# Attention probabilities by values in float32 with two heads in column halves, and one pool of four PSUM banks

## The chip, the cores and the metric

The kernel runs on one core of a Trainium2 chip. A core has five engines that run side by side, each with its own queue taken in order: TensorE (PE in the profile, its weight loads PEld), VectorE (DVE), ScalarE (ACT), GpSimd (POOL) and SyncE (SP), which here only issues transfers. Matmul results land in PSUM, eight banks of 512 float32 a partition; everything else lives in SBUF, 128 partitions. The metric is device time of one execution, in microseconds (us).

## What is computed

Threshold attention over 8 batches, 8 heads, 576 positions of 64 channels, and behind it a feed-forward part on the 512 channels of a position. Cut to what matters:

```python
scores = scale * q @ k.T                       # per head, 576 x 576
thresh = max(scores, axis=-1) - tau
p = where(scores >= thresh, exp(scores - max), 0)
attn = p / (sum(p) + 1e-9)
x = attn @ v                                   # heads side by side: 8 x 576 x 512
xk = mu_k * x + (1 - mu_k) * x_prev            # x_prev: the position before
xr = mu_r * x + (1 - mu_r) * x_prev
k = maximum(xk @ w_k, 0)                       # 512 -> 1024
out = sigmoid(xr @ w_r) * ((k * k) @ w_v)
```

The weights arrive as float64 words and are converted on the chip.

## The kernel before

**Number formats.** Outside batch 0 a float32 operand is split into a rounded part (`hi`, float32r) and the rest (`lo`), and a product is taken as hi x hi + hi x lo + lo x hi in the faster float32r form. The first eight jobs are `plain`: float32 throughout.

**Attention.** A job is a pair of heads of one batch (`hp`); batch 0 is cut into two rounds of four half jobs. `operands` (L397) loads q and k, scales q, splits (ScalarE L433, GpSimd L439) and stacks them by transfers into `st1`, `st2`; the values are loaded as `vraw` and split into `vs` (ScalarE L481, GpSimd L489). A unit is two query tiles of 128 rows of one head (kind P), or the last 64 rows of both heads (kind T, with the block-diagonal operand `bd`, GpSimd L528). `softmax` (L576) takes each query tile (128 x 576 scores, two banks of the tag `s`) through maximum (DVE L599), threshold (ACT L607), exponent (ACT L615), mask with row sum (DVE L623), inverse (DVE L633, L634) and scaling (POOL L648) into `p`. `turn_pair` (L693) and `turn_last` (L756) transpose `p` on TensorE (L670, banks of the tag `pt`) and evict each bank twice: `upper` rounds on ScalarE (L681) into `phi`, `lower` subtracts on VectorE (L687) into `plo`. `attend` (L809) multiplies by `vs` for one head: 9 matmuls with 128 output columns of the array (L860), where one half of the output holds the product with the rounded values and the other the product with their rest. ScalarE copies one half (L872) and VectorE adds the halves into `xT` (L880), or `xE` for the last 64 rows (L894). Plain jobs multiply in float32 (L823).

**Feed-forward.** `ffn_chunk` (L916) takes 256 positions at a time, 18 chunks. It mixes (difference POOL L958, scale ACT L966, sum POOL L975, rounding ACT L981, rest POOL L989), multiplies by `w_k` (L1011), takes relu, square, rounding and rest into `k2` (L1019 to L1034, through the tile `r`), multiplies by `w_r` (L1053), takes the sigmoid (L1061), multiplies by `w_v` (L1075), gates (DVE L1081) and stores. Its products and the output of `attend` use banks of the tag `w`.

**Weights.** `weight` (L317) converts each of 20 pieces: absolute value (ACT L340), clip (POOL L348), three bit operations (DVE L362, L369, L379), rounding (ACT L386) and rest (POOL L390), with `xT[1]` as scratch.

**Order.** Every step is recorded with an engine, an estimated duration, what it reads and writes, and a key. `Plan.order` (L108) simulates the engines: at each step it takes the ready step that can start first, ties by the smaller key, and writes out the order in which all are issued. Attention's TensorE steps have keys 1000 lower, so the feed-forward part fills what attention leaves. A tile of a tag takes that tag's buffers in turn: the n-th waits for the release of the one `bufs` before it. PSUM's eight banks: `s` two tiles of two banks, `pt` two, `w` two.

## Time and profile before

| | us |
|---|---|
| median of 3 runs (lowest, highest) | 1181.38 (1179.02, 1182.25) |
| the profiled execution | 1178.11 |
| its span, first to last instruction | 1176.3 |

| engine | busy us | share of the span |
|---|---|---|
| PE | 1084.4 | 92% |
| PEld | 932.4 | 79% |
| ACT | 906.4 | 77% |
| DVE | 860.7 | 73% |
| POOL | 748.7 | 64% |

The mean granted clock of TensorE is 0.978 of full speed. A line of the profile's groups reads: line of the kernel, engine, operation, tile written <- tiles read, shapes, count | busy us, mean ns of one | idle time of that engine just before them and what ended it. Matmuls are pipelined, and the records' ends are modelled, so the rate of a stream of matmuls is read from start to start, not from the duration of a record.

### The profile page before, as it was taken

Reading aid. Unit: us, or ns where it says so; the run is one execution under the profiler, and the core shown is the slowest. Engines: PE = TensorE matmul, PEld = TensorE weight load, DVE = VectorE, ACT = ScalarE, POOL = GpSimd, SP = SyncE. Lnnn points to the kernel's source line nnn. Section 1 sums busy time; section 2 is a strip of 40 time slices with the busy share of each in tenths; the row PEclk is TensorE's granted clock in tenths of the full one; section 3 lists DMA queues with packets and bytes.
Section 4 is the critical chain, followed back from the end, with each engine's and each line's share of the span. In section 5 each row is a group of like instructions: output and inputs, shape, how many; then the busy total and the mean of one; then the engine's idle time right before and its main releaser. Section 6 shows DMA issues by size and latency. Waiting matters only on the chain.

```text
span 1176.3 us, 20089 instructions
## 1 busy us (share of the span) xinstructions
PE 1084.4 (92%) x6728; PEld 932.4 (79%) x6728; DVE 860.7 (73%) x2013; ACT 906.4 (77%) x1918; POOL 748.7 (64%) x854
## 2 busy tenths in 40 slices
PE   6788899997999889997999999999999999998998
PEld 4455678886988778986988888979788888887897
DVE  4678767889778877888878797878787787887100
ACT  4678678887779788887888887878788888875643
POOL 1889865656766476646675766656667676653661
PEclk9789899999999999999999999999999999998999
DMA  6552203434443324244343342434434334220000
GB/s 240 165 206 82 42 22 89 100 105 104 97 113 93 96 57 113 73 94 114 86 114 96 102 108 47 108 82 97 104 96 108 84 82 114 69 56 19 9 28 18
DMA packets 36806, 106.82 MB, mean 91 GB/s; under 512 B 5984, under 2 KB 5984, under 8 KB 36704
## 3 DMA queue, kind: packets, MB, share of 16 engines
q1 hardware_dynamic: 36704, 105.54, 34.5%
q8 instruction: 54, 0.88, 0.3%
q14 instruction: 48, 0.39, 0.1%
HBM read 44.70 MB, written 9.44 MB: 46 GB/s over the span
## 4 chain that ended last, share of the span: by engine, by line
PE 50%; ACT 16%; DVE 16%; POOL 11%; issue 5%; DMA 2%; SPq 0%; POOLq 0%; DVEq 0%; ACTq 0%
PE w L1011 11%; PE s L566 8%; PE pt L670 8%; PE w L1075 7%; PE w L1053 6%; PE w L860 6%; DVE p L623 5%; POOL p L648 4%; ACT p L615 3%; ACT phi L681 3%; DVE plo L687 3%; DVE sm L599 3%; PE w L823 2%; PE s L544 2%; DVE phi L687 2%
## 5 line engine op out<-in xcount | busy, mean ns | idle before, releaser
L648 POOL TENSOR_SCALAR p<-p,sm 128x576 f32<-128x576 f32 x288 | 216.8, 761 | 222.0 <-DVE sm L634 202.7
L681 ACT ACTIVATE phi<-pt 128x512 fp32r<-128x512 f32 (+6 forms) x528 | 227.4, 458 | 65.2 <-PE pt L670 60.8
L623 DVE SCALAR_TENSOR_TENSOR p<-s,sm,p 128x576 f32<-128x576 f32 x288 | 232.8, 815 | 59.1 <-ACT p L615 53.5
L1011 PE MATMUL w<-xk,wk 128*128 128x256 f32 x1728 | 252.3, 291 | 2.3 <-POOL xk L989 1.1
L670 PE MATMUL pt<-ident,p 128*128 128x128 f32 x1312 | 216.7, 281 | 39.0 <-POOL p L648 28.5
L599 DVE TENSOR_REDUCE sm<-s 128x1 f32<-128x576 f32 x288 | 211.7, 751 | 49.9 <-PE s L544 28.9
L1011 PEld LDWEIGHTS w<-xk,wk 128*128 128x128 f32 x1728 | 226.8, 194 | 5.9 <-issue 1.9
L670 PEld LDWEIGHTS pt<-ident,p 128*128 128x128 f32 x1312 | 155.6, 142 | 85.3 <-POOL p L648 52.5
L1075 PE MATMUL w<-wv,k 128*128 128x512 f32 x864 | 221.2, 398 | 0.2 <-ACT sg L1057 0.2
L615 ACT ACTIVATE p<-s,sm 128x576 f32<-128x576 f32 x288 | 211.9, 736 | 1.1
L687 DVE TENSOR_TENSOR plo<-pt,phi 128x512 fp32r<-128x512 f32 x280 | 172.4, 632 | 54.7 <-ACT phi L681 52.4
L1075 PEld LDWEIGHTS w<-wv,k 128*128 128x128 f32 x864 | 155.3, 189 | 28.6 <-ACT sg L1057 0.4
L860 PE MATMUL w<-phi,vs 128*128 128x320 f32 (+1 forms) x560 | 157.0, 303 | 2.0 <-ACT r L1019 1.4
L607 ACT ACTIVATE sm<-sm,small 128x1 f32<-128x1 f32 x288 | 83.9, 291 | 60.9 <-DVE sm L599 59.2
L860 PE MATMUL w<-plo,vs 128*128 128x320 f32 (+1 forms) x448 | 124.7, 300 | 2.9 <-DVE plo L687 2.6
L566 PE MATMUL s<-st 128*128 128x288 f32 x448 | 106.1, 318 | 13.3 <-DVE p L623 12.0
L1034 POOL TENSOR_TENSOR k<-r,k 128x512 fp32r<-128x512 f32 x72 | 92.9, 1290 | 38.3 <-ACT k L1024 38.3
L1053 PE MATMUL w<-wr,xk 128*128 128x512 f32 x432 | 115.3, 401 | 0.0
L860 PEld LDWEIGHTS w<-phi,vs 128*128 128x128 f32 x560 | 105.6, 189 | 5.4 <-ACT r L1019 2.0
L566 PE MATMUL s<-st,st 128*128 128x288 f32 x448 | 97.7, 299 | 0.0
L566 PEld LDWEIGHTS s<-st 128*128 128x128 f32 x448 | 71.3, 190 | 32.2 <-DVE p L623 23.3
L439 POOL TENSOR_TENSOR lo<-raw,hi 128x576 fp32r<-128x576 f32 (+1 forms) x56 | 83.6, 1498 | 18.8 <-ACT hi L433 17.3
(78 smaller groups left out, 1636.7 us busy)
## 6 DMA issues: line engine op xcount, KB each, us to landing
raw<-in_qk SPq DMA_DIRECT2D x28, 608.0 KB, 5.0
st<-hi SPq DMA_DIRECT2D x56, 304.0 KB, 3.3
st<-lo SPq DMA_DIRECT2D x56, 304.0 KB, 4.3
vraw<-in_v SPq DMA_DIRECT2D x28, 320.0 KB, 3.1
out<-sg SPq DMA_DIRECT2D x32, 256.0 KB, 2.0
st<-hi SPq DMA_DIRECT2D x56, 144.0 KB, 3.7
st<-lo SPq DMA_DIRECT2D x56, 144.0 KB, 4.1
st<-in_qk SPq DMA_DIRECT2D x8, 608.0 KB, 5.0
```

What stands on the lines that cost most here:

```text
L566: PE.matmul(s.get()[:, z, 0:HS], lt, r.get()[:, k0 + z * HS : k0 + (z + 1) * HS], start=(j == 0), stop=(j == len(prods) - 1),)
L599: lambda sv=sv, col=col: V.tensor_reduce(col(0), sv(), axis=AX.XY, op=ALU.max, negate=True),
L615: lambda sv=sv, pv=pv, col=col: A.activation(pv(), sv(), AF.Exp, bias=col(0)),
L623: lambda sv=sv, pv=pv, col=col: V.scalar_tensor_tensor(pv(), sv(), col(1), pv(), op0=ALU.is_ge, op1=ALU.mult, accum_out=col(2)),
L648: lambda y=y: G.tensor_scalar(p.get()[:, y], p.get()[:, y], sm.get()[:, 3, y : y + 1], 0.0, op0=ALU.mult, op1=ALU.add),
L670: lambda c=c, o=o: PE.transpose(pt.get()[:, c, :], p.get().rearrange("p y s -> p (y s)")[:, o : o + P], ident.get()),
L681: add("ACT", occ, lambda: A.activation(out_(), in_(), AF.Copy), reads=[pt], writes=w, key=key)
L687: lambda: V.tensor_tensor(out_(), in_(), hi_().bitcast(F32), op=ALU.subtract),
L860: lambda j=j, c=c, m=m: PE.matmul(o.get()[:, 0:n], vs.get()[:, c], m.get()[:, c, 0:n], start=(j == 0), stop=(j == len(prods) - 1)),
L1011: PE.matmul(h.get()[:, f], l, r, start=(ct == 0 and i == 0), stop=(ct == NCT - 1 and i == 2))
L1053: PE.matmul(z.get(), l, r, start=(ct == 0 and i == 0), stop=(ct == NCT - 1 and i == 2))
L1075: PE.matmul(vps.get(), l, r, start=(ft == 0 and i == 0), stop=(ft == NFT - 1 and i == 2))
```

## The change

- The split of probabilities and values goes: `phi`, `plo`, `vs`, `upper`, `lower` are replaced by `pm`, `pl` and `v` in float32 for all jobs. `attend` runs once for both heads of a query half: head 0 writes output rows 0 to 63 of one bank (array columns 0 to 63) and head 1 rows 64 to 127, with float32 matmuls that alternate between the heads.
- A P unit is one query tile of both heads. A plain unit's scores are issued for both heads as one step, heads alternating; they write both `s` tiles.
- A transposed bank is evicted once: the first on ScalarE, the second on VectorE (on ScalarE too up to key 40). One eviction on VectorE takes the product to `xT`, one more to `xE`.
- `bd` is filled on ScalarE, the weights' clip is on VectorE, and in the mixing two operations (scale, sum) become one VectorE operation.
- The tags `pt` and `w` become one of four banks. A tile takes any free buffer of its tag, the one free longest, in place of the next in turn. `r` has one buffer in place of two, `raw` two in place of one.
- Some TensorE steps now record a write to the SBUF tile that their result will be evicted to (`pm`, `pl`, `xT`, `k2`, `sg`), so that they wait for its release themselves.
- A job's order is T, 0, 1, 2, 3 (before: P, T, P, P, P).

```diff
-                h = held[b.tag]
-                if len(h) >= b.bufs:
-                    o = h[-b.bufs]
-                    if left[id(o)]:
-                        return None
-                    t = max(t, freed[id(o)] + self.HOP)
+                h = sorted(freed[id(o)] if o else -1.0 for o in held[b.tag] if not (o and left[id(o)]))
+                if len(h) <= m:
+                    return None
+                t = max(t, h[m] + self.HOP)
...
+    EV = ("ACT", 0.49), ("DVE", 0.6)
...
-            "POOL",
-            0.7,
-            lambda: G.tensor_scalar(t(), t(), W_MIN, W_MAX, op0=ALU.max, op1=ALU.min),
+            "DVE",
+            0.46,
+            lambda: V.tensor_scalar(t(), t(), W_MIN, W_MAX, op0=ALU.max, op1=ALU.min),
...
+        raw = job["raw"] = sbuf("raw", [P, W], F32, 2)
...
+        vt = job["v"] = sbuf("v", [P, 5, P], F32, VB)
...
-                        "POOL",
-                        0.21,
-                        lambda v=v, src=src, sl=sl: G.tensor_scalar(
-                            bd.get()[sl, v, sl], src.get()[sl, SM:S].bitcast(F32), 1.0, 0.0, op0=ALU.mult, op1=ALU.add
+                        "ACT",
+                        0.104,
+                        lambda v_=v_, src=src, sl=sl: A.activation(
+                            bd.get()[sl, v_, sl], src.get()[sl, SM:S].bitcast(F32), AF.Copy
...
+            def both():
                 for z in range(2):
+                    for h in range(2):
+                        hr = slice(h * D, (h + 1) * D)
+                        o = ss[1].get()[hr, z, 0:HS] if last else ss[h].get()[:, z, 0:HS]
+                        q = slice(SM, S) if last else slice(c * P, (c + 1) * P)
+                        PE.matmul(o, raw.get()[hr, q], raw.get()[hr, keys(h, z)], start=True, stop=True)
...
-        pt = psum("pt", [P, 4, P], 2)
+        pt = psum("w", [P, 4, P], 4)
...
+            pt = transposes(p, (y,), [y * (S + ST) + j * P for j in range(4)], n + y - 1.0, [(pm, (y, c % 2))])
+            evict(
+                *EV[y if n > EARLY else 0],
                 pt,
+                lambda y=y: pm.get()[:, y, :, cs],
                 lambda pt=pt: pt.get(),
...
+        pt = transposes(p, (0, 1), [SM], n + 0.1, [(pl, c % 2)])
+        evict("ACT", 0.2, pt, lambda: pl.get()[:, cs], lambda: pt.get()[:, 0], [(pl, c % 2)], n - 1.0)
...
+            for c in range(4):
+                for h in range(2):
+                    hs = slice(h * D, (h + 1) * D)
+                    PE.matmul(o.get()[hs, 0:n], vt.get()[:, c, hs], pm.get()[:, h, c, 0:n], start=(c == 0), stop=False)
+            for h in range(2):
+                hs = slice(h * D, (h + 1) * D)
+                PE.matmul(o.get()[hs, 0:n], vt.get()[:, 4, hs], pl.get()[:, 0:n], start=False, stop=True)
...
+        free = [(x, (hp, g))] + ([(xE, (b % NE, hp))] if n > CH else [])
+        add("PE", occ, mm, reads=[vt, pm, pl], writes=[o, *free], key=key - 1000, lat=occ + 0.2)
+        evict(
             "DVE",
...
-                        A.activation(
-                            d.get()[:, y], diff.get()[:, y], AF.Copy, scale=mu_sb.get()[:, j, hc + y : hc + y + 1]
-                        )
...
-                        G.tensor_tensor(mo, mo, prv[:, cs], op=ALU.add)
...
+                            V.scalar_tensor_tensor(
+                                d.get()[:, y, o : o + n],
+                                diff.get()[:, y, o : o + n],
+                                mu_sb.get()[:, j, hc + y : hc + y + 1],
+                                prv[:, hc + y],
+                                op0=ALU.mult,
+                                op1=ALU.add,
+                            )
...
-            h = psum("w", [P, 2, CH], 2)
+            h = psum("w", [P, 2, CH], 4)
...
-            r = sbuf("r", [P, 512], F32, 2)
+            r = sbuf("r", [P, 512], F32, 1)
```

On the host the values are laid out so that the last 64 positions of head 0 stand in rows 0 to 63 with zeros below them in its columns, and those of head 1 in rows 64 to 127 with zeros above, so that one tile `pl` serves both heads.

More of the change, by code (lines that the diff above doesn't have):

```diff
@@ L186, in order @@
                     placed.add(id(b))
-                    held[b.tag].append(b)
+                    h = held[b.tag]
+                    idle = [j for j, o in enumerate(h) if not (o and left[id(o)])]
+                    b.slot = min(idle, key=lambda j: freed[id(h[j])] if h[j] else -1.0)
+                    h[b.slot] = b
                     turn[b.tag] += 1
@@ L500, in scores, with keys @@
-    def scores(unit, y, s, key):
-        job = unit["job"]
-        k0 = KT + (ST if unit["kind"] == "P" and y == 0 else 0)
-        if unit["kind"] == "T" and job["plain"]:
-            raw = job["raw"]
-            for z in range(2):
-                def both(z=z):
-                    for h in range(2):
-                        hr = slice(h * D, (h + 1) * D)
-                        PE.matmul(
-                            s.get()[hr, z, 0:HS],
-                            raw.get()[hr, SM:S],
-                            raw.get()[hr, k0 + z * HS : k0 + (z + 1) * HS],
-                            start=True,
-                            stop=True,
-                        )
-                add("PE", 0.6, both, reads=[raw], writes=[(s, z)], key=key - 1000, lat=0.9)
-            return
-        if unit["kind"] == "T":
+    def scores(unit, ss, key):
+        job, c = unit["job"], unit["c"]
+        raw = job["raw"]
+        def keys(y, z):
+            k0 = KT + (ST if unit["kind"] == "P" and y == 0 else 0)
+            return slice(k0 + z * HS, k0 + (z + 1) * HS)
+        if unit["kind"] == "T" and not job["plain"]:
@@ new lines, in scores, with mm @@
+            for j, (v_, r) in enumerate(prods):
+                def mm(j=j, v_=v_, r=r):
+                    for z in range(2):
+                        PE.matmul(ss[1].get()[:, z, 0:HS], bd.get()[:, v_], r.get()[:, keys(1, z)], start=(j == 0), stop=(j == 2))
+                add("PE", 0.264, mm, reads=[bd, r], writes=[ss[1]], key=key - 1000, lat=0.44)
+            return
+        if unit["kind"] == "T" or job["plain"]:
+            last = unit["kind"] == "T"
+            def both():
+                for z in range(2):
+                    for h in range(2):
[3 more added lines that the diff above has]
+                        PE.matmul(o, raw.get()[hr, q], raw.get()[hr, keys(h, z)], start=True, stop=True)
+            occ = 1.2 if last or key > COLD else 2.3
+            add("PE", occ, both, reads=[raw], writes=list(ss.values()), key=key - 1000, lat=occ + 0.25)
+            return
@@ new lines, in scores, with mm @@
+        for y in range(2):
+            st1, st2 = job["st"][y]
+            for j, l in enumerate((st1, st2)):
+                def mm(j=j, l=l, r=st1, y=y):
+                    for z in range(2):
+                        PE.matmul(
+                            ss[y].get()[:, z, 0:HS],
+                            l.get()[:, c * P : (c + 1) * P],
+                            r.get()[:, keys(y, z)],
+                            start=(j == 0),
+                            stop=(j == 1),
+                        )
+                add("PE", 0.264, mm, reads=[l, st1], writes=[ss[y]], key=key + 0.5 * y - 1000, lat=0.44)
@@ L654, in softmax, with group, transposes @@
             )
-    def group(job, h, g):
-        if (h, g) not in job["groups"]:
-            job["groups"][h, g] = (
-                sbuf("phi", [P, 5, 320], F32 if job["plain"] else FR, 2),
-                sbuf("plo", [P, 4, 320], FR, 2),
-            )
-        return job["groups"][h, g]
-    def transposes(p, y, at, key):
-        pt = psum("pt", [P, 4, P], 2)
+    def group(job, g):
+        if g not in job["groups"]:
+            job["groups"][g] = (
+                sbuf("pm", [P, 2, 4, CH + ST], F32, 2),
+                sbuf("pl", [P, CH + ST], F32, 2),
+            )
+        return job["groups"][g]
+    def transposes(p, y, at, key, to):
+        pt = psum("w", [P, 4, P], 4)
         for c, o in enumerate(at):
@@ new lines, in turn_last @@
+        cs = slice(CH, CH + ST)
+        pt = transposes(p, (1,), [S + ST + c * P for c in range(4)], n - 1.0, [(pm, (0, 2)), (pm, (1, 2))])
+        evict(
+            "ACT",
+            0.5,
+            pt,
+            lambda: pm.get()[:, :, :, cs],
+            lambda: pt.get().rearrange("p c (h q) -> p h c q", h=2),
+            [(pm, (0, 2)), (pm, (1, 2))],
+            n - 2.0,
+        )
+        pe = transposes(p, (1,), [S], n - 0.9, [(pl, (2, 0)), (pl, (2, 1))])
+        for h in range(2):
+            evict(
+                "ACT",
+                0.13,
+                pe,
+                lambda h=h: pl.get()[h * D : (h + 1) * D, cs],
+                lambda h=h: pe.get()[0:D, 0, h * ST : (h + 1) * ST],
+                [(pl, (2, h))],
```

446 lines of the change are left out of this document (94 added, 352 removed).

## The prediction

> **What bounds the kernel now.** I read the stages first, then TensorE's own groups in the long middle stage, then the rates at which its matmuls start. The first fence gives each stretch: length, busy time of TensorE, its weight loads, VectorE, ScalarE and GpSimd (instructions in brackets), granted clock, DMA share, GB/s.
>
> ```profile
> 0.00:180.00 180.00, 151.14 (x627) 99.64 (x627) 122.48 (x232) 121.47 (x275) 131.41 (x119) 0.91 0.39 127
> 180.00:1085.00 905.00, 846.97 (x5588) 755.35 (x5586) 731.66 (x1770) 742.21 (x1571) 572.43 (x682) 0.99 0.37 91
> 85.00:155.00 70.00, 60.64 (x290) 40.31 (x290) 58.56 (x105) 51.57 (x122) 64.08 (x51) 0.93 0.22 64
> ```
>
> Three stages with three answers. Up to about 180 us the first batch's attention runs beside the conversion of the weights, and in its later part (85 to 155) GpSimd is busy 64.1 of 70 us. From 180 to 1085 TensorE is busy 94%, with ScalarE at 82% and VectorE at 81%. After 1085 three chunks of the feed-forward part follow one another.
>
> ```profile
> 1115.96 11.62 PE L1011 MATMUL w<-xk,wk 128*128 128x256 f32 x96
> 1127.41 5.63 PE L1053 MATMUL w<-wr,xk 128*128 128x512 f32 x24
> 1132.88 11.05 PE L1075 MATMUL w<-wv,k 128*128 128x512 f32 x48
> 1143.77 11.62 PE L1011 MATMUL w<-xk,wk 128*128 128x256 f32 x96
> ```
>
> Rows of the timeline (start, length, instructions merged). From start to start, a chunk is 27.8 us of matmuls without a gap, so the last 90 us are TensorE alone. They also give clean rates: 11.45/96 = 0.119 us for L1011, 5.47/24 = 0.228 for L1053, 10.89/48 = 0.227 for L1075. How full is the middle stage by such rates?
>
> ```profile
> L1011 PE MATMUL w<-xk,wk 128*128 128x256 f32 x1351 | 199.5, 290 | 1.2 <-DVE xT L880 0.8 <-ACT xk L981 0.4
> L1075 PE MATMUL w<-wv,k 128*128 128x512 f32 x720 | 188.0, 400 | 0.2 <-ACT sg L1057 0.2
> L670 PE MATMUL pt<-ident,p 128*128 128x128 f32 x1128 | 183.7, 277 | 27.4 <-POOL p L648 18.6 <-DVE plo L687 7.1 <-ACT p L615 0.7
> L860 PE MATMUL w<-phi,vs 128*128 128x320 f32 (+1 forms) x555 | 155.8, 303 | 2.0 <-ACT r L1019 1.4 <-DVE sg L1081 0.6
> L860 PE MATMUL w<-plo,vs 128*128 128x320 f32 (+1 forms) x444 | 123.7, 300 | 2.9 <-DVE plo L687 2.6
> L566 PE MATMUL s<-st 128*128 128x288 f32 x440 | 104.2, 318 | 13.3 <-DVE p L623 12.0
> L566 PE MATMUL s<-st,st 128*128 128x288 f32 x440 | 96.0, 300 | 0.0
> L1053 PE MATMUL w<-wr,xk 128*128 128x512 f32 x348 | 95.1, 403 | 0.0
> L566 PE MATMUL s<-hi,bd 128*128 128x288 f32 x108 | 26.2, 325 | 10.3 <-DVE p L623 10.2
> L566 PE MATMUL s<-lo,bd 128*128 128x288 f32 x54 | 12.7, 318 | 0.0
> ```
>
> Groups of 180 to 1085: count, busy us, mean ns, then idle time before them and its releasers. The idle stands before transposes (L670, waiting for GpSimd's scaled probabilities) and before scores (L566, waiting for VectorE's mask at L623 to give a score bank back). The remaining rates come from these stretches of the timeline (the row without an operation's name is from the chain of waits):
>
> ```profile
> 166.20 0.42 PE L566 MATMUL s<-st,st 128*128 128x288 f32 x2
> 166.46 1.78 PE L823 MATMUL w<-phi,vs 128*128 128x320 f32 x6
> 168.08 0.60 PE L670 MATMUL pt<-ident,p 128*128 128x128 f32 x4
> 168.51 1.44 PE L823 MATMUL w<-phi,vs 128*128 128x320 f32 x4
> 345.30 1.33 PE w L860 x9
> 1094.41 0.28 PE L860 MATMUL w<-phi,vs 128*128 128x256 f32 x1
> ...
> 1095.35 0.28 PE L860 MATMUL w<-phi,vs 128*128 128x256 f32 x1
> ```
>
> Start to start: scores 0.26/2 = 0.13 us, float32 attention by values (L823, 320 columns) 1.62/6 = 0.27, transposes 0.43/4 = 0.108, split attention (L860) 1.33/9 = 0.148 at 320 columns and 0.94/8 = 0.118 at 256. Counts times rates: 161 (L1011) + 163 (L1075) + 79 (L1053) + 122 (transposes) + 133 (L860, at the mean of its two widths) + 136 (scores) = 794 us. So 111 of 905 us are not filled by matmuls at their rate. That is what the change can win in the middle. What it adds to 794 it pays in full.
>
> **Part 1: attention by values in float32, in column halves.** Each float32 product shows as two records, as L823 does. Before, a job (head pair) of batches 1 to 7 issues 18 records at 320 columns and 18 at 256: 18 x (0.148 + 0.118) = 4.79 us. After, it issues 20 + 20 records of 64 columns of output each, at 0.27 and, by width, 0.216 us. If the two heads' halves overlap, 10 x 0.486 = 4.86 us: +0.07 a job, +2 us in 28 jobs. If they do not, 9.72: +138 us. The trace has no two matmuls on the same rows and different columns. The nearest row is the score of the last tile, four records in two diagonal quarters:
>
> ```profile
> 86.03 0.70 PE L510 MATMUL s<-st 64*64 64x288 f32 x4 [2.03 <-DVE p L623]
> 86.67 1.14 PE L670 MATMUL pt<-ident,p 128*128 128x128 f32 x8
> ```
>
> Four records of 288 columns (0.243 us each by L823's rate) would need 0.97 us in a row; they took 0.64 until the next matmul started, and two overlapped pairs need 0.49. So quarters overlap, and 0.16 us is lost, which I take as the price of going into the tiled form and out of it. I take overlap for the halves too (nearest row), with 0.16 us for each of 56 groups, +9. Sum: **+11 us**, bounds +2 and +147.
>
> The Trainium skill, "TensorE: Matmul & The Clock Gate", Part 3, measured speedup against the span model, gives 2.38 times for three column tiles, not 3. At that share (0.79) two halves would give 1.59 times and, as an estimate, 6.1 us a job or +37 us. The rows above show overlap of quarters at 0.97/0.64 = 1.5 times with the entry in it, but no run so far shows column halves.
>
> **Part 2: what leaves the other engines.**
>
> ```profile
> L687 DVE TENSOR_TENSOR plo<-pt,phi 128x512 fp32r<-128x512 f32 x224 | 150.9, 686 | 51.0 <-ACT phi L681 49.1
> L687 DVE TENSOR_TENSOR phi<-pt,phi 64x128 fp32r<-64x128 f32 x224 | 64.6, 288 | 22.8 <-ACT phi L681 17.8
> L880 DVE TENSOR_TENSOR xT<-w,r 64x256 f32<-64x256 f32 x112 | 46.9, 419 | 31.2 <-ACT r L872 29.1
> L681 ACT ACTIVATE phi<-pt 128x512 fp32r<-128x512 f32 x224 | 131.0, 594 | 35.0 <-PE pt L670 32.7
> L966 ACT ACTIVATE mk<-m,mu_sb 128x256 f32<-128x256 f32 x72 | 32.7, 502 | 21.7 <-POOL m L958 21.6
> L489 POOL TENSOR_TENSOR vs<-vraw,vs 128x320 fp32r<-128x320 f32 x56 | 49.2, 879 | 38.8 <-ACT vs L481 36.6
> L975 POOL TENSOR_TENSOR mk<-mk,xT 128x512 f32<-128x512 f32 x32 | 38.7, 1209 | 16.8 <-ACT mk L966 16.8
> ```
>
> Per P unit the two 512-wide evictions were one ScalarE copy and one VectorE subtraction each; now one goes to each engine. ScalarE: 112 copies less (-66 us), the mixing's scale of L966 gone for both mixes (-65). VectorE: 224 subtractions become 112 copies, at most 0.686 us each (-74); the subtractions of the tails go (-65); adding the two heads becomes one copy for both heads (-23). It gains the mixing: 128 fused operations of 256 columns and 64 of 64. The trace has none of these; the nearest row is L880 at 256 columns, 0.419, so 54 to 80 us. It also gains the 20 weight clips, 0.686 by the 512-wide row, +14. Net VectorE **-70 to -95**, ScalarE **at least -130**, GpSimd -49 (L489) and -77 (L975, two mixes). The small copies for the last tile's scores (bd) go to ScalarE, 112 of them, ahead of a unit's exponents in its queue; at no more than 0.502 (L966's row) they are 56 us, inside the 130. Without that cover TensorE's scores would wait 0.5 us for each. So in the middle ScalarE comes from 82% to 68 to 74%, VectorE from 81% to 70 to 73%.
>
> These engines do not set the end; what counts is the wait before TensorE. The waits named above pass through VectorE and ScalarE queues that were four fifths full. One of the two evictions that a transposed bank waited for is gone, and the `lower` step behind it too. What is late next: the chain maximum, exponent, mask, GpSimd scale itself, which the change leaves as it is. I take 60 of the 111 us as won: bounds 0 (all of it is that chain's latency) and 100.
>
> The other edits I cost at nothing. One pool of four banks holds what two pools of two held. The relu tile `r` in one buffer puts relu, square, round and subtract of a block in a row: three ScalarE passes (0.594 as L681) and one of GpSimd (1.21 as L975), 3.0 us against 2.9 of L1011 for the block. With four banks TensorE runs ahead, and the last block's chain, 3.4 us past L1011's end, lies under the 5.5 us of L1053; without that cover, 3.4 x 18 chunks = 61 us. Matmuls and transposes now wait for `k2`, `sg`, `pm` and `xT` themselves, with the next scores queued behind them and VectorE waiting for those; but what they wait for is TensorE's own earlier work, a store, or mixing of two batches before. Bytes loaded stay the same, and `raw` gets a second buffer.
>
> **Part 3: the start.**
>
> ```profile
> L348 POOL TENSOR_SCALAR xT<-xT 128x512 f32<-128x512 f32 x20 | 39.5, 1989 | 0.4 <-ACT xT L340 0.2
> 131.22 7.56 POOL L348 TENSOR_SCALAR xT<-xT 128x512 f32<-128x512 f32 x4
> 140.24 1.33 PE L670 MATMUL pt<-ident,p 128*128 128x128 f32 x5 [3.51 <-POOL p L648]
> ```
>
> The clip costs GpSimd 1.99 us apiece. Four in a row from 131.22 to 138.78 hold the scaled probabilities back, and TensorE sits idle 3.51 us. On VectorE they are 14 us where 39.5 were. VectorE itself is busy 58.6 of 70 us in 85 to 155, though, and gets some 7 us there, so of those 70 us at most 5 to 10 go by this alone. Beside that, the float32 products of batch 0 overlap: L823's 160 records, near 0.243 each, fall from 39 to 20 us, and the scores of two heads on different rows overlap as well. From 141 us TensorE is packed, so a good part of the 19 counts there. I take **-24**, bounds -5 and -45. After 1085 nothing changes: 0.
>
> **The sum.** It is made against the profiled execution, 1178.1 us (span 1176.3 and 1.8 around it), 3.3 below the median of the runs, 1181.4: 1178.1 + 11 - 60 - 24 = 1105; I add 3 for the median: **1108 us**.
>
> **The rivals.**
>
> - *More than half is won.* Every gap in the middle but 15 us closes, and the start gives 40: 1178 + 11 - 96 - 40 = 1053 to about 1075. For it: stretches without attention, the last three chunks, have no gap at all. Chance 0.17.
> - *Each pair of halves pays the 0.16/2 us*, not each group: 0.08 x 20 pairs x 28 jobs = 45 in place of 9, so 1108 + 36 = 1144. The skill's 2.38 for three tiles would come to nearly the same. Chance 0.08.
> - *The waits are latency, not queues.* The same chain from L599 to L648 stands between scores and transposes, so the middle keeps its gaps: 1178 + 11 - 20 = 1169, or up to 1180 if a bank of the shared pool is missing for a transpose. For it: GpSimd, the last releaser, was never the full engine in the middle (63%). Chance 0.11.
> - *Column halves run one after the other*, the other side: 20 records of 0.486 us in a row, +138 instead of +2, and no gain for batch 0's products (about 10): 1108 + 136 + 10 = 1254. It turns the sign once more than half of each pair's second half is exposed (73 of 138 us is what the rest wins). For it: no row has the same rows and other columns. Against it: quarters overlap. That would also be the change not doing what it says. Chance 0.10.
>
> **How the numbers follow.** Forecast (1080 to 1135) 0.54, and the rivals as given, 0.17, 0.08, 0.11, 0.10. The range must leave out no more than 0.2: from 1060 (most of the first rival) to 1176 (most of the third); the serial halves stay out. Faster by over 0.3%, about what a measurement of this kernel can tell from no change: 0.54 + 0.17 + 0.08 + most of the third, 0.86; within 0.3%: 0.04; slower: 0.10.
>
> **What would show it.** In the changed kernel's profile, starts of two column-half records a few ns apart, then one pair every 0.27 us at 320 columns; if 0.54, the last rival holds. ScalarE and VectorE under 75% from 200 to 1000 us and idle before transposes and scores under half of today's 51 us (27.4 + 13.3 + 10.3); if idle stays with VectorE and ScalarE emptier, the third holds. No GpSimd run of 7 us before 150 us, and the first L1011 of batch 0 before 141 us. The last three chunks still 27.8 us each. What would make the prediction wrong in size is the 60: it is read from how full the engines were, not from a row.

## The result, and the profile after

| | median us (lowest, highest) | ratio to before, 95% interval |
|---|---|---|
| before, same chip | 1180.2 (1177.23, 1182.25), 4 runs | |
| the changed kernel | 1137.39 (1136.06, 1139.91), 4 runs | 0.9642 [0.9613, 0.967] |

The change makes the kernel faster by 43 us; 72 had been forecast. The profiled execution took 1139.91 us with a span of 1137.8, against 1176.3 before.

First the page of the changed kernel: busy time by engine, and the granted clock in 40 slices.

```profile
PE 1047.7 (92%) x6840; PEld 850.9 (75%) x6840; DVE 770.0 (68%) x1703; ACT 725.4 (64%) x1532; POOL 554.7 (49%) x570
...
PEclk8767998999999999999999999999999999999999
```

ScalarE lost 181 us of work, GpSimd 194, VectorE 91, and TensorE is still 92% busy. The span shrank far less than the work of the others, so the rest is a matter of where TensorE waits. The stages of the changed kernel, columns as in the prediction:

```profile
20.00:85.00 65.00, 37.48 (x169) 24.59 (x170) 64.05 (x117) 40.64 (x80) 36.28 (x31) 0.71 0.48 173
85.00:155.00 70.00, 62.44 (x360) 45.37 (x359) 46.53 (x96) 44.32 (x90) 33.17 (x32) 0.88 0.14 46
...
180.00:1045.00 865.00, 832.01 (x5646) 684.15 (x5646) 617.83 (x1384) 582.52 (x1255) 439.14 (x459) 0.99 0.39 93
```

And of the kernel before, the stretch that the prediction did not show:

```profile
20.00:85.00 65.00, 55.21 (x181) 34.27 (x181) 43.68 (x79) 43.70 (x93) 50.27 (x42) 0.82 0.52 177
```

Two things stand out. In the middle VectorE is now at 71% and ScalarE at 67%. In 20 to 85 us TensorE does less than before, 37.48 us against 55.21, while VectorE has become the full engine: 64.05 of 65 us. The granted clock there is lower too, 0.71 where it was 0.82.

**Do the halves overlap?** The timeline of TensorE in the changed kernel, and beneath it starts of single records in ns from the same trace:

```profile
176.50 2.37 PE L690 MATMUL w<-pm,v 128*64 128x320 f32 x16
178.70 0.71 PE L693 MATMUL w<-pl,v 128*64 128x320 f32 x4
179.34 0.76 PE L617 MATMUL w<-ident,p 128*128 128x128 f32 x5
...
606.28 2.42 PE L690 MATMUL w<-pm,v 128*64 128x256 f32 x16 [2.72 <-DVE pm L631]
608.48 1.07 PE L693 MATMUL w<-pl,v 128*64 128x256 f32 x4
...
610.62 0.62 PE L509 MATMUL s<-st 128*128 128x288 f32 x2
```

```
L690, 256 columns: 606767 606774 | 606983 606990 | 607199 607206 | 607415 607422 | 607631 607643 | 608057 608070
L509, 288 columns: 609487 609895 610135 610375 610615 610855, and L617 from 611074
```

The two heads' records start 7 ns apart and a pair goes every 0.216 us (0.268 at 320 columns): two for the time of one. From 176.50 to 179.34 the ten pairs of a group take 2.84 us, 2.68 of them the pairs; the 0.16 left is lost at the group's start and end.

**How full is the middle?** The groups of TensorE in 180 to 1045 of the changed kernel:

```profile
L829 PE MATMUL w<-xk,wk 128*128 128x256 f32 x1344 | 186.8, 285 | 0.2 <-ACT pm L629 0.2
L893 PE MATMUL w<-wv,k 128*128 128x512 f32 x652 | 171.3, 399 | 1.1 <-DVE sg L899 0.9 <-DVE xE L631 0.2
L617 PE MATMUL w<-ident,p 128*128 128x128 f32 x1144 | 169.2, 278 | 13.7 <-POOL p L592 11.2 <-DVE sg L899 1.0
L690 PE MATMUL w<-pm,v 128*64 128x320 f32 (+1 forms) x896 | 123.7, 417 | 4.9 <-DVE pm L631 2.7 <-DVE sg L899 1.2 <-ACT pl L629 1.0
L509 PE MATMUL s<-st 128*128 128x288 f32 x444 | 105.1, 319 | 13.0 <-DVE p L567 7.3 <-issue 4.9 <-PE s L509 0.6
L509 PE MATMUL s<-st,st 128*128 128x288 f32 x444 | 98.3, 303 | 0.0
L871 PE MATMUL w<-wr,xk 128*128 128x512 f32 x336 | 87.9, 397 | 0.0
L693 PE MATMUL w<-pl,v 128*64 128x320 f32 (+1 forms) x224 | 37.8, 410 | 0.0
L484 PE MATMUL s<-hi,bd 128*128 128x288 f32 x108 | 24.3, 306 | 0.0
L484 PE MATMUL s<-lo,bd 128*128 128x288 f32 x54 | 11.8, 301 | 0.0
```

By the prediction's rates, with 560 pairs at 0.242 us (the mean of both widths): 160 + 148 + 124 + 135 + 136 (scores) + 77 = 780 of 865 us. So 85 us are not filled, where 111 of 905 were. The idle that the profile names before transposes and scores went from 51 to 13.7 + 13.0 = 26.7, and 4.9 new before the products.

For the experiments I take the same sum batch by batch: unfilled time is the length of a stage less its matmuls times their start-to-start rate (records that run beside another counted once). It holds idle time, and also what is lost when the granted clock is low. A stage ends at the last row maximum (L543, L599 before) of a batch. In us:

| | start to end of batch 0: length / unfilled | batch 1: length / unfilled | batches 2 to 7: unfilled | behind: unfilled | TensorE's work |
|---|---|---|---|---|---|
| before | 162.2 / 68.8 | 120.9 / 15.3 | 90.2 | 11.9 | 990 |
| after | 167.6 / 87.2 | 106.2 / 23.8 | 61.9 | 7.7 | 957 |

The span's 38.5 us are thus 33 of work (35 less in batch 0, 2 more elsewhere) and 5.6 of unfilled time: +18.4 in the start, +8.5 in batch 1, -28.3 in batches 2 to 7, -4.2 behind them. Nearly all that the middle got back from its gaps was lost again ahead of it. A part of that loss is the clock. The granted clock is 0.84 up to 168 us, where it was 0.90 up to 163 before, and 0.95 in batch 1 where it was 1.00. If the slow stretches run at half clock, as the one in the last section does, 0.95 of 106 us is some 10 us of them, so about 5 of the 8.5 us in batch 1, as an estimate.

The last row maximum now comes at 974.6 us (before 1076.7), so five chunks run behind attention where it was three:

```profile
1033.33 5.67 PE L871 MATMUL w<-wr,xk 128*128 128x512 f32 x24
1038.84 11.05 PE L893 MATMUL w<-wv,k 128*128 128x512 f32 x48
1049.72 10.48 PE L829 MATMUL w<-xk,wk 128*128 128x256 f32 x87
```

The next two chunks start at 1077.5 and 1105.3: 27.8 us each, as before.

### The profile page after: what moved, and what is told of

The parts are those of the page before. It is cut to its first block, busy times and chain, and to the rows that moved or that the text cites. A ratio compares the mean times of both kernels' runs of the same rounds, so it can differ in the third digit from the quotient of the medians.

```text
span 1137.8 us, 19250 instructions
## 1 busy us (share of the span) xinstructions
PE 1047.7 (92%) x6840; PEld 850.9 (75%) x6840; DVE 770.0 (68%) x1703; ACT 725.4 (64%) x1532; POOL 554.7 (49%) x570
## 4 chain that ended last, share of the span: by engine, by line
PE 62%; DVE 20%; ACT 9%; POOL 3%; issue 3%; DMA 2%; SPq 1%; POOLq 0%; DVEq 0%; ACTq 0%
PE w L829 14%; PE w L893 11%; PE w L617 10%; PE s L509 8%; PE w L690 8%; PE w L871 6%; DVE p L567 5%; DVE mk L786 5%; DVE sm L543 3%; ACT p L559 2%; PE w L693 2%; DVE sm L577 2%; POOL p L592 2%; PE s L484 2%; PE s L498 1%
## 5 line engine op out<-in xcount | busy, mean ns | idle before, releaser
L592 POOL TENSOR_SCALAR p<-p,sm 128x576 f32<-128x576 f32 x288 | 220.9, 779 | 287.9 <-DVE sm L578 195.5
L543 DVE TENSOR_REDUCE sm<-s 128x1 f32<-128x576 f32 x288 | 210.9, 751 | 47.3 <-PE s L509 29.2
L829 PE MATMUL w<-xk,wk 128*128 128x256 f32 x1728 | 235.0, 285 | 0.2 <-ACT pm L629 0.2
L617 PE MATMUL w<-ident,p 128*128 128x128 f32 x1312 | 200.8, 285 | 25.9 <-POOL p L592 23.2
L829 PEld LDWEIGHTS w<-xk,wk 128*128 128x128 f32 x1728 | 218.1, 190 | 2.0 <-issue 0.8
L617 PEld LDWEIGHTS w<-ident,p 128*128 128x128 f32 x1312 | 153.6, 145 | 77.2 <-POOL p L592 54.6
L629 ACT ACTIVATE pm<-w 128x512 f32<-128x512 f32 x178 | 105.2, 592 | 110.3 <-PE w L617 109.7
L690 PE MATMUL w<-pm,v 128*64 128x256 f32 (+1 forms) x1024 | 146.8, 426 | 4.9 <-DVE pm L631 2.7
L852 POOL TENSOR_TENSOR k<-r,k 128x512 fp32r<-128x512 f32 x72 | 93.3, 1296 | 85.4 <-ACT k L842 79.8
L786 DVE SCALAR_TENSOR_TENSOR mk<-m,mu_sb,xT 128x256 f32<-128x256 f32 x128 | 79.6, 662 | 80.7 <-POOL xk L807 80.4
L807 POOL TENSOR_TENSOR xk<-mk,xk 128x512 fp32r<-128x512 f32 x72 | 93.3, 1296 | 70.0 <-ACT xk L799 66.7
L690 PEld LDWEIGHTS w<-pm,v 128*64 128x64 f32 x1024 | 74.8, 142 | 59.6 <-issue 11.1
L509 PE MATMUL s<-st 128*128 128x288 f32 x448 | 106.3, 319 | 13.9 <-DVE p L567 7.3
L509 PE MATMUL s<-st,st 128*128 128x288 f32 x448 | 99.4, 304 | 0.0
L509 PEld LDWEIGHTS s<-st 128*128 128x128 f32 x448 | 72.6, 193 | 34.7 <-issue 17.0
```

Of the source, the lines that this page charges most:

```text
L509: PE.matmul(ss[y].get()[:, z, 0:HS], l.get()[:, c * P : (c + 1) * P], r.get()[:, keys(y, z)], start=(j == 0), stop=(j == 1),)
L543: lambda sv=sv, col=col: V.tensor_reduce(col(0), sv(), axis=AX.XY, op=ALU.max, negate=True),
L592: lambda y=y: G.tensor_scalar(p.get()[:, y], p.get()[:, y], sm.get()[:, 3, y : y + 1], 0.0, op0=ALU.mult, op1=ALU.add),
L617: lambda c=c, o=o: PE.transpose(pt.get()[:, c, :], p.get().rearrange("p y s -> p (y s)")[:, o : o + P], ident.get()),
L629: fn = lambda: A.activation(out_(), in_(), AF.Copy)
L690: PE.matmul(o.get()[hs, 0:n], vt.get()[:, c, hs], pm.get()[:, h, c, 0:n], start=(c == 0), stop=False)
```

## The experiments

| run | edit | median us | ratio to before, 95% |
|---|---|---|---|
| e1_clip_pool | after, clip back on GpSimd | 1154.62 | 0.9787 [0.976, 0.9814] |
| e6_before_clip | before, clip on VectorE | 1182.83 | 1.0017 [1.0001, 1.0034] |
| e5_plain_apart | after, batch 0's scores one step a head | 1113.55 | 0.9443 [0.9396, 0.949] |
| e9_coupled_serial | after, one step, issued head after head | 1146.71 | 0.9717 [0.9684, 0.975] |
| e3_serial | after, halves issued head after head | 1249.09 | 1.0585 [1.0548, 1.0622] |
| e2_mix_old | after, mixing as before | 1123.82 | 0.9525 [0.95, 0.955] |
| e8_mk2 | after, `mk` in two buffers | 1121.07 | 0.9493 [0.9467, 0.9519] |
| e12_evict_act | after, both evictions on ScalarE | 1138.34 | 0.9652 [0.9634, 0.9671] |
| e4_pools | after, banks in two pools | 1127.37 | 0.9547 [0.952, 0.9574] |
| e7_prices | after, measured durations in the plan | 1162.15 | 0.984 [0.9814, 0.9866] |
| e10_apart_mk2 | e5 and e8 | 1127.56 | 0.9544 [0.9518, 0.9569] |
| e11_apart_mk2_pools | e5, e8 and e4 | 1124.69 | 0.9523 [0.9497, 0.9549] |

Unfilled TensorE time by stage, as defined above:

| | to the end of batch 0 | batch 1 | batches 2 to 7 | behind |
|---|---|---|---|---|
| after | 167.6 / 87.2 | 23.8 | 61.9 | 7.7 |
| e1 | 184.6 / 104.2 | 23.3 | 59.9 | 7.2 |
| e6 | 150.7 / 58.5 | 28.3 | 93.2 | 11.2 |
| e5 | 152.9 / 71.4 | 9.6 | 52.3 | 4.3 |
| e9 | 174.1 / 93.9 | 24.3 | 61.6 | 7.9 |
| e3 | 185.9 / 95.7 | 26.8 | 70.7 | 5.2 |
| e2 | 166.4 / 86.1 | 24.2 | 48.2 | 5.2 |
| e8 | 162.2 / 83.3 | 20.7 | 53.3 | 5.0 |
| e12 | 165.8 / 85.4 | 22.8 | 67.1 | 4.9 |
| e4 | 166.2 / 85.8 | 25.1 | 52.9 | 5.0 |
| e7 | 171.6 / 91.2 | 34.1 | 65.8 | 12.0 |
| e10 | 158.0 / 73.9 | 22.5 | 52.7 | 4.4 |
| e11 | 156.8 / 76.2 | 16.6 | 54.7 | 4.4 |

Every edit makes the planner write a new order, so a difference holds the edit and its order together. How much the order weighs can be read where an edit touches the start alone: batches 2 to 7 give 61.9, 59.9 and 61.6 (after, e1, e9) and 90.2 and 93.2 (before, e6). There, differences of 8 us mean something.

### The start: the clip

e1_clip_pool:

```diff
-            "DVE",
-            0.46,
-            lambda: V.tensor_scalar(t(), t(), W_MIN, W_MAX, op0=ALU.max, op1=ALU.min),
+            "POOL",
+            0.7,
+            lambda: G.tensor_scalar(t(), t(), W_MIN, W_MAX, op0=ALU.max, op1=ALU.min),
```

> The changed kernel with one part undone: the weights' clip back on GpSimd. Theory S: in the changed kernel VectorE is the full engine of the start (busy 64.05 of 65 us from 20 to 85 us), so the clip's move gave back there what it won on GpSimd. It then expects VectorE to drop by about 10 us in that stretch, GpSimd to rise by 20 or so, and the total within 6 us of 1137. Rival: the move of the clip is what shortened the start; then the total rises by 15 us or more.

Measured: 17.2 us slower than the changed kernel, nearly all of it in the start (batch 0 ends at 184.6 us, not 167.6). Two windows of e1:

```profile
20.00:85.00 65.00, 37.64 (x145) 23.74 (x145) 52.64 (x87) 34.22 (x68) 57.81 (x39) 0.68 0.39 145
85.00:155.00 70.00, 51.00 (x291) 35.70 (x290) 46.62 (x86) 38.08 (x81) 41.68 (x34) 0.80 0.17 57
```

The clip only changes which engine is nearly full at first: VectorE gets 11 us back, GpSimd is at 57.81 of 65. More of the conversion then falls into 85 to 155 (8 of its subtractions at L390, where it was 5), where TensorE is busy 51.00 us against 62.44. In this kernel the clip's move is worth 17 us.

e6_before_clip makes the opposite edit in the kernel before (the same three lines, POOL to DVE).

> The kernel before with one part of the change alone: the weights' clip on VectorE. The prediction's start (GpSimd full in 85 to 155 us, clips in its way) expects -5 to -20 us against 1180. Theory S (VectorE is close behind, 58.6 of 70 us there) expects the small end, 0 to -8.

Measured: +2 us, no change that counts. Three windows of e6:

```profile
20.00:85.00 65.00, 57.18 (x220) 36.35 (x221) 54.18 (x107) 49.53 (x106) 36.63 (x37) 0.92 0.54 191
85.00:155.00 70.00, 64.66 (x310) 43.95 (x309) 60.48 (x109) 53.27 (x129) 43.18 (x40) 0.93 0.19 52
155.00:290.00 135.00, 118.25 (x708) 97.81 (x708) 100.39 (x246) 97.83 (x212) 69.83 (x87) 1.00 0.38 91
```

And the last of them in the kernel before:

```profile
155.00:290.00 135.00, 125.35 (x778) 106.09 (x776) 107.30 (x265) 107.39 (x237) 75.37 (x93) 1.00 0.37 91
```

Batch 0 ends 11.5 us earlier, but batch 1 leaves 13 us more unfilled: from 155 to 290 TensorE is busy 118.25 us where it was 125.35. Here the earlier end of one batch was no gain, since the next left more of its gaps unfilled.

### The start: both heads' scores in one step

The changed kernel's timeline of TensorE in the start:

```profile
39.29 3.04 PE L498 MATMUL s<-raw 64*128 64x288 f32 x8 [5.46 <-issue]
...
61.43 1.29 PE L498 MATMUL s<-raw 64*128 64x288 f32 x2 [6.81 <-issue]
63.65 2.26 PE L498 MATMUL s<-raw 64*128 64x288 f32 x6 [0.93 <-DVE p L567]
...
82.82 3.04 PE L498 MATMUL s<-raw 64*128 64x288 f32 x8 [4.61 <-issue]
```

The long idle times stand before L498, the step that now writes both `s` tiles. At 61.43 its first two records run, and the others then wait for VectorE's mask of the other tile. Is it the coupling that costs? e5_plain_apart takes the step apart; e9_coupled_serial keeps it as one step, issues head 0's matmuls and then head 1's, and was meant to give up the overlap.

```diff
+            if not last:
+                for h in range(2):
+
+                    def one(h=h):
+                        hr = slice(h * D, (h + 1) * D)
+                        for z in range(2):
+                            PE.matmul(
+                                ss[h].get()[:, z, 0:HS], raw.get()[hr, c * P : (c + 1) * P], raw.get()[hr, keys(h, z)], start=True, stop=True
+                            )
+
+                    occ = 1.0 if key > COLD else 1.9
+                    add("PE", occ, one, reads=[raw], writes=[ss[h]], key=key + 0.5 * h - 1000, lat=occ + 0.25)
+                return
```

> The changed kernel, but batch 0's score products of the two heads are two steps, one per head, each writing its own score tile (no overlap of the heads on TensorE, no wait for both score tiles at once). Theory S2: a part of the start is lost because a unit's scores wait until both score tiles of the unit before are masked; then the total falls by 3 to 12 us although TensorE gets 15 us more work in batch 0. Rival: the overlap of the two heads' scores is what counts: total up by 5 us or more.

```diff
-                for z in range(2):
-                    for h in range(2):
+                for h in range(2):
+                    for z in range(2):
...
-            occ = 1.2 if last or key > COLD else 2.3
+            occ = 2.0 if last or key > COLD else 3.8
```

> The changed kernel, but batch 0's score step (both heads in one step, as in the change) issues head 0's products and then head 1's, so that they do not overlap; priced accordingly in the plan. It tells the two halves of the run before with separate steps (1113.6 us) apart. Theory S2 (waiting for both score tiles at once is what cost the start): this one gains nothing, 1135 to 1155. Rival (the alternating products themselves cost more than they save, for instance by changing TensorE into a tiled form): 1112 to 1125, as with separate steps.

Measured: 1113.55 apart, 1146.71 with one step issued head after head, where the changed kernel (one step, heads alternating) has 1137.39. But e9 did not give up the overlap. A step of e9:

```profile
129.65 1.25 PE L498 MATMUL s<-raw 64*128 64x288 f32 x8
```

Eight records in 1.25 us; one after the other they need 8 x 0.243 = 1.94. By the starts of their records (time at half clock counted half) the 16 such steps take 20.1 us in the changed kernel, 22.1 in e9 and 29.1 in e5, where 15.6 is full overlap and 31.1 none. So e9 differs from the changed kernel in the order of the heads and in the plan's price of the step, not in overlap, and the 9.3 us between them are not the overlap's.

What the runs do show is the merged step: 24 or 33 us slower than e5, whichever way the heads are issued, so the alternation is not what costs. That is the range theory S2 gave for e9, though e9 did not do what S2 took it to do. Batch 0 ends at 152.9 us in e5, 167.6 in the changed kernel and 174.1 in e9, with 71.4, 87.2 and 93.9 us unfilled. The idle time that the profiles put before this step, up to 180 us, is 18.4, 36.7 and 35.5 us. Most of the difference has no releaser in the profile ("issue": 1.1 us of it in e5, 20.2 in the changed kernel). That the plan places a merged step only once both `s` tiles are free fits this, but is argued from the plan's code. The start of e5:

```profile
20.00:85.00 65.00, 52.66 (x187) 29.75 (x186) 60.81 (x116) 41.87 (x88) 35.64 (x30) 0.72 0.49 177
```

TensorE runs 187 matmuls here where the changed kernel ran 169, with VectorE at 60.81 of 65 us: a nearly full VectorE alone did not hold it back. Behind batch 0, e5 is ahead of e9 by 14.7 us of unfilled time in batch 1 (granted clock 1.00 against 0.95), 9.3 in batches 2 to 7 and 3.6 after them. In e10, which has the same edit, batch 1 does not show it (22.5). I take batch 0's unfilled time, 16 us against the changed kernel in the table (9 if scores are counted by their starts), as the coupling's, and leave open how much of the rest is the order that came with it.

### The middle: is it latency, or the queues?

e3_serial issues the two heads of a product one after the other, to test the prediction's last rival, and doubles the plan's price for it.

```diff
-            for c in range(4):
-                for h in range(2):
-                    hs = slice(h * D, (h + 1) * D)
-                    PE.matmul(o.get()[hs, 0:n], vt.get()[:, c, hs], pm.get()[:, h, c, 0:n], start=(c == 0), stop=False)
...
+                for c in range(4):
+                    PE.matmul(o.get()[hs, 0:n], vt.get()[:, c, hs], pm.get()[:, h, c, 0:n], start=(c == 0), stop=False)
...
-        occ = 10 * 0.842e-3 * n + 0.2
+        occ = 20 * 0.842e-3 * n + 0.2
```

> The changed kernel with the products by values issued head after head (all of head 0, then all of head 1) in place of alternating, and priced double in the plan. Theory W (the total is TensorE's work plus a nearly fixed unfilled remainder, so each us of TensorE work counts): +138 us in batches 1 to 7 and 20 in batch 0, total 1280 to 1300. Rival: the other engines bound the middle and TensorE has room; then under 1240.

Measured: +112 us, and slower than the kernel before, so the overlap carries the sign of the whole change. But this edit took away only a part of the overlap. A group of e3:

```profile
612.68 2.42 PE L690 MATMUL w<-pm,v 128*64 128x320 f32 x10
614.89 0.43 PE L691 MATMUL w<-pl,v 128*64 128x320 f32 x1
614.94 0.43 PE L690 MATMUL w<-pm,v 128*64 128x320 f32 x1
...
617.19 1.21 PE L617 MATMUL w<-ident,p 128*128 128x128 f32 x9
```

L691 ends a head's products, so the L690 at 614.94, beside head 0's first L691, is head 1's, though it was issued behind. In the starts, four records of head 1 run beside the last four of head 0. The group takes 4.51 us; 20 records in a row would take 5.36, and the changed kernel takes 2.84 (at 256 columns e3 takes 3.65, the changed kernel 2.31). That is 3.0 us for each of 32 pairs of groups, some 96 us in all and not 138 + 20. The table counts 16 steps a group for e3; by it, e3 has 92 us more work and 18 more unfilled than the changed kernel, 70.7 in batches 2 to 7 where it was 61.9. So the added work was paid in full and no gap closed under it. Theory W, with the work that was really added, gives 1137 + 92 = 1229 us; the rival, that TensorE has room in the middle, is not borne out.

e2_mix_old puts the mixing back on ScalarE and GpSimd, e8_mk2 keeps it fused on VectorE and gives its tile a second buffer, e12_evict_act takes the 75 us of evictions off VectorE instead.

```diff
-                d = sbuf("mk", [P, 2, CH], F32, 1)
+                d = diff if j == 1 else sbuf("mk", [P, 2, CH], F32, 1)
...
+                        A.activation(
+                            d.get()[:, y], diff.get()[:, y], AF.Copy, scale=mu_sb.get()[:, j, hc + y : hc + y + 1]
+                        )
...
+                        G.tensor_tensor(mo, mo, prv[:, cs], op=ALU.add)
```

> The changed kernel with one part undone: the mixing as before (scale on ScalarE, sum on GpSimd, two buffers in effect). Theory Q (the middle's gain comes from emptier queues on ScalarE and GpSimd): ScalarE +65 us, GpSimd +90, VectorE -99; unfilled TensorE time from 180 us to the end of attention rises from 75 us towards 104, total 1150 to 1165. Rival: the fused operations on VectorE cost more than they relieve (662 ns each where the nearest row said 419, and they wait 102 us for the one buffer mk); then the total falls by 5 us or more.

```diff
-                d = sbuf("mk", [P, 2, CH], F32, 1)
+                d = sbuf("mk", [P, 2, CH], F32, 2)
```

> The changed kernel with two buffers for the mixing's tile mk in place of one. VectorE's fused mixing step waits 102 us in all for GpSimd to release that one buffer, with the softmax of later units queued behind it. Theory: most of that wait falls behind the end of attention, where VectorE has nothing else to do, so within 4 us of 1137. Rival: it holds up the softmax in the middle: 1127 or less.

```diff
-    EV = ("ACT", 0.49), ("DVE", 0.6)
+    EV = ("ACT", 0.49), ("ACT", 0.49)
```

> The changed kernel with both transposed banks of a unit evicted on ScalarE in the later batches too (110 copies of 0.686 us leave VectorE, 110 of 0.592 us come to ScalarE). Taking the mixing off VectorE gave 14 us, but that run also had two mixing buffers. Theory V: the load of VectorE itself is what TensorE's remaining gaps in batches 2 to 7 (62 us) follow; then they fall to 45 to 55 and the total to 1120 to 1132. Rival: it was the single mixing buffer, and VectorE's load does not matter at this level; then the gaps stay at 58 or more, with ScalarE fuller, and the total at 1134 or more.

Measured: e2 -13.6 us, e8 -16.3, e12 +1. The same 670 us in the middle, first of the changed kernel, then e2, e8 and e12:

```profile
280.00:950.00 670.00, 646.98 (x4446) 530.78 (x4445) 506.13 (x1135) 464.90 (x1014) 349.05 (x367) 0.99 0.43 102
```

```profile
280.00:950.00 670.00, 655.91 (x4560) 543.71 (x4559) 454.02 (x1049) 506.97 (x1126) 403.93 (x429) 1.00 0.43 103
```

```profile
280.00:950.00 670.00, 656.99 (x4556) 542.40 (x4554) 521.43 (x1177) 472.28 (x1035) 353.25 (x375) 0.99 0.42 102
```

```profile
280.00:950.00 670.00, 649.15 (x4435) 533.78 (x4434) 438.73 (x1016) 501.48 (x1086) 349.80 (x366) 0.99 0.41 100
```

The third column of times is VectorE. It falls to 438.73 in e12 and nothing is won; it rises to 521.43 in e8 and 10 us more of TensorE fit in. ScalarE and GpSimd are busier in e2 than in the changed kernel, and that is faster too. So in this range no engine's load alone sets the middle; in e12 the rival of its forecast held. What e2 and e8 have in common is that one mix no longer waits until the tile of the other has been read. The waits of the changed kernel, then of e8 (total us, times, longest):

```profile
DVE mk L786 <- POOL xk L807: 102.3, 30, 13.6
```

```profile
DVE mk L786 <- POOL xk L807: 84.7, 18, 13.5
```

Twelve waits, 18 us in all, are gone; in each, whatever stood behind in VectorE's queue waited too. During attention this wait falls from 21.8 to 6.1 us; the rest comes after attention has ended and costs nothing. So theory and rival of e8 were both right in part: most of the wait lies behind, and the little in the middle counts. One thing speaks against a tidy conclusion: e5 has one `mk` buffer and 52.3 us unfilled in batches 2 to 7, e10 has two and 52.7. So the buffer's 8.6 us depend on the order that is written around it.

e4_pools cuts the four banks into two for transposes and two for the rest (five lines like these):

```diff
-        pt = psum("w", [P, 4, P], 4)
+        pt = psum("pt", [P, 4, P], 2)
...
-        o = psum("w", [P, 512], 4)
+        o = psum("w", [P, 512], 2)
```

> The changed kernel with the PSUM pool cut again into two of two banks (transposes, everything else). By the prediction the one pool costs and gains nothing: within 5 us of 1137. Rival: the shared pool is what closes gaps before transposes and scores: 1150 or more. Other rival: sharing starves the transposes: 1130 or less.

Measured: -10 us, 9 of them in batches 2 to 7. The shared pool does not help here; the prediction had it at nothing. The time is the one that the other rival named, but not for its reason: from 180 to 960 us idle before transposes is 12.2 us in the changed kernel and 13.8 in e4, while before scores (L509) it falls from 12.8 to 7.8 and before products from 4.9 to 1.4.

e7_prices writes measured durations into the plan for some thirty steps; the first of them:

```diff
-    EV = ("ACT", 0.49), ("DVE", 0.6)
+    EV = ("ACT", 0.59), ("DVE", 0.69)
```

> The changed kernel with the plan's estimated durations of VectorE, ScalarE and GpSimd steps set to the durations that its profile shows (exponent 0.735 for 0.625, mask 0.90 for 0.74, inverse 0.49 for 0.29, mixing 0.97 for 0.70, and so on); nothing else is touched. Theory L: the unfilled time left in the middle (75 us from 180 us to the end of attention) is an order written from too short estimates, so TensorE reaches transposes and scores too early: total 1105 to 1125. Rival (latency or queues that no order avoids): within 6 us of 1137.

Measured: +25 us, which neither theory nor rival had. Attention's last row maximum comes at 1062 us where it was 975, and all four stages have more unfilled. But this run has a lower granted clock, 0.943 to 0.946 in all four executions, where the changed kernel has 0.966 to 0.973. Batch 1 and batches 2 to 7 of the changed kernel, then of e7:

```profile
168.00:274.00 106.00, 94.24 (x621) 76.00 (x621) 77.20 (x182) 73.42 (x167) 49.72 (x54) 0.95 0.44 108
274.00:975.00 701.00, 677.64 (x4664) 556.82 (x4660) 531.20 (x1189) 487.24 (x1060) 365.50 (x386) 1.00 0.42 100
```

```profile
172.00:288.00 116.00, 99.61 (x620) 82.25 (x620) 77.55 (x181) 74.60 (x167) 50.52 (x54) 0.87 0.41 99
288.00:1062.00 774.00, 750.91 (x5074) 626.83 (x5074) 543.41 (x1217) 525.21 (x1109) 392.33 (x407) 0.98 0.38 92
```

If every slow stretch is at half clock, 0.943 of 1160 us is 132 us of them and 0.968 of 1138 us is 73: 59 more, which cost up to 30 us of matmuls, as an estimate. The span grew by 22, with the same work. So e7 does not tell whether too low prices cost the middle its time: what it lost, the clock can account for. Why the clock was lower under this order is not shown.

e10 and e11 put together what had helped.

> Two repairs together: batch 0's score products of the two heads as separate steps, and two buffers for mk. If the two act in different stages (start and second batch for the first, later batches for the second), they add: 1113.6 - 9 = 1105, or 1100 to 1110. If both only shift the same order, no better than 1113.

> The two repairs and the PSUM pool cut into two of two banks. If each pool's effect in the later batches (9 us) stands by itself: 1092 to 1101. If the shared pool's loss came from the same gaps that the second mk buffer closed: equal to the run with two repairs, within 4 us.

Measured: 1127.56 and 1124.69. Gains of 23.8 (e5), 16.3 (e8) and 10 (e4) taken alone become 9.8 and 12.7 together. Batch 0 still ends early (158.0 and 156.8 us), batches 2 to 7 stay at 53 and 55; batch 1 gives back what e5 had won there. Here too the clock has a share: 0.966 in e10 and 0.975 in e5 are, by the same estimate, 21 us more at half clock, or some 10 of the 14 us between them. e5 alone, at 1113.55 us, is the fastest version found.

## Why the forecast was right in sign and too good by 29 us

- **Attention in column halves, +11: right.** Full overlap, +2 of work, and 0.16 us for a group's entry and exit, as measured above. The last rival's price, 146 us for serial halves (136 and 10), was not put to the test: in e3, which cost 112, a part of each group still overlapped. The Trainium skill, "TensorE: Matmul & The Clock Gate", Part 3, measured speedup against the span model, gives 2.38 times for three column tiles; here two tiles give 0.43 us of records in 0.216, twice. By that share (2.38/3 = 0.79) ten pairs at 256 columns would, as an estimate, take 2.7 us, not 2.16. The measurement decides.
- **The start, -24: -17, from other terms.** TensorE's work fell by 35 us (products 19, as said, and scores 16 at full overlap, which the forecast named and didn't price) and unfilled time rose by 18. By the starts, scores really fell by 10; the rest is in the 18. In the changed kernel the clip was worth 17 us (e1), not 5 to 10, and nothing in the kernel before (e6). Without the merged step, e5 has 71.4 us unfilled, close to the 68.8 before; with it there are 87.2, and batch 0 ends 14.7 us later although TensorE has 9 us less of scores to do. The step that failed is "the scores of two heads on different rows overlap as well": it counted a gain and did not ask what the merged step waits for, two `s` tiles free at once, of two in all.
- **The middle, -60: the step that failed.** With the 9 us for entries, which lie in unfilled time as well, -51 was expected; 8.5 - 28.3 - 4.2 = -24 came. The 60 was "read from how full the engines were, not from a row", and that reading fell: e2 and e12 take 52 and 67 us of 506 off VectorE, and only e2 gains, where a wait went too. What the remaining 62 us in batches 2 to 7 are is not settled. If they were the softmax chain's latency, as in the third rival, more TensorE work in each unit should cover them; in e3 it did not, though that run has an order of its own. No edit came below 48. Which parts of the change won the 28 us is not shown either: no run undoes the single eviction of a bank, the new unit, the choice of any free buffer, or the new order of a job's units.
- **Edits costed at nothing.** The shared pool cost 10 us in this order (e4), and the fused mixing's single `mk` buffer, at which the forecast didn't look, 16 (e8). Their gains did not add (e10, e11).
- **Price of the mixing, 54 to 80 us: low.** Groups of the changed kernel:

```profile
L786 DVE SCALAR_TENSOR_TENSOR mk<-m,mu_sb,xT 128x256 f32<-128x256 f32 x128 | 79.6, 662 | 80.7 <-POOL xk L807 80.4
L631 DVE COPY pm<-w 128x512 f32<-128x512 f32 x110 | 75.5, 686 | 32.7 <-PE w L617 32.4
L786 DVE SCALAR_TENSOR_TENSOR mk<-m,mu_sb,xE 128x64 f32<-128x64 f32 x64 | 19.6, 376 | 21.9 <-POOL xk L807 21.9
L348 DVE TENSOR_SCALAR xT<-xT 128x512 f32<-128x512 f32 x20 | 11.4, 584 | 0.0
```

  79.6 + 19.6 = 99 us. The price left out what GpSimd does beside it: where GpSimd was idle, a fused operation of 256 columns took 0.48 us (last section), so 128 of them 61. The copies were 0.686 as taken, the clip 11.4 where 14 was taken, `bd` 28 where 56 was the bound. VectorE at 71% and ScalarE at 67% in the middle came out near the forecast (70 to 73, 68 to 74); it did not decide the time.
- **Behind attention, 0: right in rate.** A chunk still takes 27.8 us; that five of them come last and not three was not foreseen and changes nothing by itself.
- **What would show it.** Starts and rates of the pairs, both engines under 75% and the last chunks came as written. Named idle came to 26.7, just over the half of 51 that was asked for, and the shortfall in time says the same. The first matmul by `w_k` of batch 0 told nothing: it stood at 104.4 us before and at 104.9 after.

## What to carry to other kernels

How full the other engines are (here 82 and 81%) didn't tell what lighter ones would win: look for the single waits that hold up a queue, as the one before `mk`. When an edit is to take an overlap away, look in the starts whether it did: here twice, matmuls issued head after head still ran side by side. Compare the granted clock of two orders before calling their difference gaps. When two steps are merged for overlap, count the buffers that the merged step needs free at once before counting the overlap. And where a planner rewrites the order, one edit's gain need not add to another's: run the sum as well as the parts, and trust a stage only where it repeats under edits made elsewhere.

## What the hardware showed that was not expected

- The fused mixing of 256 columns varies widely. The view of its line (minimum, median, maximum ns):

```profile
L786 DVE SCALAR_TENSOR_TENSOR mk<-m,mu_sb,xT x128: 465/484/1715, 56.8 to 1073.3; 128x256 f32<-128x256 f32 x128
```

  The prediction's nearest row, the addition at L880, took 0.419; the median here is 0.484, some take three times as long, and the mean is 662 ns. GpSimd tells them apart: the 82 that ran with GpSimd idle took 472 to 487 ns each; of the 44 that began while GpSimd was busy, 40 took more than 600 ns, with a median of 964. The Trainium skill, "SBUF — State Buffer", Terms, says that VectorE and GpSimd share a port pair, held for a whole instruction. The trace agrees with that.
- After TensorE had sat idle for 2.72 us, pairs that had gone every 216 ns went 414 ns apart from 607.6 us on (the starts shown above), and scores 240 ns apart, where 130 is the rate elsewhere, until 611 us. The granted clock fell to half in just that stretch (third number from the end):

```profile
604.20:607.60 3.40, 1.31 (x12) 0.92 (x14) 3.40 (x7) 0.97 (x5) 0.96 (x1) 1.00 0.63 132
607.60:611.00 3.40, 3.40 (x16) 2.24 (x13) 1.01 (x6) 0.00 (x0) 1.47 (x2) 0.50 0.65 207
```

  So short idle times can cost a second time, and no term of the forecast had this. The Trainium skill, "TensorE: Matmul & The Clock Gate", Part 1, describes such a fall to half rate after an idle window of about 3.4 us; here a shorter idle time was followed by it.
- Matmuls on different columns (e3) or rows (e9) of the array overlapped without being issued in turn: in e3 the second head's records started beside the last four of the first.
